# Re-ordered first loads in a fused linear-attention and MLP kernel: parameter rows at the head of the queue, the first batch's k and v as 96 rows of six

## The chip, the cores and the metric

The kernel runs on one core of a Trainium2 chip. The metric is the device time of one execution in microseconds; where several runs are given, their median. The core has five engines that run side by side, each through its own instruction list in order: TensorE (PE) for matmuls, VectorE (DVE), ScalarE (ACT), GpSimd (POOL) and SyncE (SP), which here only issues transfers. ScalarE's list also issues a few. Sixteen DMA engines carry the transfers.

## The reference

Two layers, one after the other. The first is linear attention without a softmax, in 8 batches of 8 heads, 576 positions and a head size of 64; the second a mixer over tokens and then over channels (512 wide, 2048 hidden).

```python
kv  = einsum('bhsd,bhse->bhde', k, v)
o   = einsum('bhsd,bhde->bhse', q, kv)
rms = sqrt(mean(o * o, axis=-1, keepdims=True) + 1e-06)
x   = (o / rms * g_norm)            # heads side by side: [8, 576, 512]

a1  = alpha1 * x + beta1
u   = x + lam * einsum('ts,bsd->btd', w_tok, a1)
a2  = alpha2 * u + beta2
out = u + lam * (maximum(a2 @ w_ch1, 0.0) @ w_ch2)
```

All inputs and the output are float32.

## The kernel before

The work of one batch goes through fixed steps: k'v per head (`kv_first` for batch 0, in float32; `kv_groups` for the others), q times it with the normalisation (`qkv_groups`, L751 for batch 0 and L744 for the others on TensorE, L779 to L808 behind it), the token mix (`tok_first`, L867, for batch 0 in two halves of four heads; `tok_groups`, L836), transposes of the result (`ut_pe`, L902, for batches 0 and 1; DMA transposes later), the first channel matmul (`ch1_groups`, L950 and L964) with its ReLU on ScalarE (L941), and the second (`ch2_groups`, L986), whose result is added to x (L995) and stored. The 576 positions are four chunks of 128 (position 4p + c on partition p in chunk c) and a tail of 64. The batches overlap: while batch b is in its channel matmuls, batch b + 1 is normalised and token-mixed and batch b + 2 has its k'v.

All that is needed once comes ahead of this or between batches 0 and 1. w_tok is loaded, transposed on TensorE (L1117, L1135) and completed by a row of its column sums (L1158). The four blocks of w_ch1 are loaded and cast to bfloat16. The four blocks of w_ch2 are loaded into spare buffers (`stg`, and `kf` for the last) and multiplied by lam (L1221, sixteen products on VectorE or GpSimd, of which the last eight write one common key, `w2s`). lam, alpha1 (times lam and g_norm), g_norm and alpha2 each become a tile of 128 equal rows by a matmul with a row of ones (L1049) and a copy (`lam_bc`, `e1g_bc`, `g_bc`, `a2_bc`).

The first loads: ScalarE's queue issues the 64-position tails of k and v of batch 0 (L497, L1063) and the rows of the parameters (L1020), and alpha2 and beta2 once more as columns of 128x4 (L1026). SyncE's queue issues, for each half of the heads, k, v and q of batch 0 as 128 rows of four positions, then w_tok, w_ch1 and the rest.

No order is written by hand. A planner, the class `Prog`, takes all operations with a cost in microseconds, a priority and their dependencies, and runs through a model of time in which each engine takes the ready operation with the best priority; the order that comes out is written as the instruction lists. A transfer in the model takes its cost `dma_us` on one line of transfers if SyncE issues it, and its cost and 2.3 us alone if ScalarE does. `plan` repeats that six times, moving the priorities of what leads to the first sixteen `ch1` groups, and keeps the best. Until the first `ch1` group is placed, the planner puts a filler into TensorE's list wherever TensorE would otherwise stand in the model: a matmul on zeros whose result nobody reads (L1276). So the fillers are a fixed part of the list, and the list is followed in order, whatever the loads do on the chip.

Of the kernel before, what the change touches and what calls it, by code (L numbers as in the profile page):

```python
# [6 lines left out]
F32 = mybir.dt.float32  # L7
# [7 lines left out]
NH = 8  # L15
# [32 lines left out]
class Prog:  # L48
# [116 lines left out]
    def schedule(self):  # L165
# [66 lines left out]
        while left:  # L232
            progressed = False
            for e, q in queues.items():
                while q and free[e] <= t + 1e-9:
# [157 lines left out]
def bass_transnormer_attn__then__resmlp_affine_kernel(  # L393
# [15 lines left out]
    with ExitStack() as stack:  # L409
# [34 lines left out]
        vt0 = stg[:, 2, 0, :].rearrange("p (h d) -> p h d", h=NH)  # L444
# [16 lines left out]
        wst2 = hst[0:64, 2304:2880]  # L461

# [26 lines left out]
        def load_main(tile, key, src, b, hs, eng="SP"):  # L489
# [4 lines left out]
                dma_us=4.0 * (hs.stop - hs.start) / 8)  # L494

        def load_tail(tile, key, src, b, lo, eng="SP"):
            P.op(eng, 0.6, lambda e: e.dma_start(  # L497
                tile[lo:lo + 64, :, :], src[b, :, 512:576, :].rearrange("h s d -> s h d")),
                w=[key], dma_us=0.8)

        HALVES = (slice(0, 4), slice(4, 8))
        ALL = (slice(0, 8),)

# [92 lines left out]
        def kv_first():  # L596

            def group(a):
                t = P.ptile(1)

                def f(e):
                    for c in range(5):
                        for h in range(4 * a, 4 * a + 4):
                            o = t.flat(slice(64 * (h % 2), 64 * (h % 2) + 64))[
                                :, 64 * (h // 2 - 2 * a):64 * (h // 2 - 2 * a) + 64]
                            m = e.matmul(o, kf[:, h, c, :] if c < 4 else kft[0:64, h, :],
                                         vf[:, h, c, :] if c < 4 else vt0[0:64, h, :],
                                         start=(c == 0 and h < 4 * a + 2), stop=(c == 4),
                                         skip_group_check=True)
                    return m  # L610
                P.op("PE", 1.6, f, r=[("kf", a), ("vf", a), "kft", ("stg", 2)], w=[t])
# [364 lines left out]
        def ch2_groups(b):  # L976
# [31 lines left out]
            for c, n in order:  # L1008
# [4 lines left out]
        params = ((g_norm, prow2[:, 0:64], g_bc, "g"), (moe_alpha1, prow[:, 0:512], e1g_bc, "e1"),  # L1013
                  (moe_lam, prow[:, 512:1024], lam_bc, "lam"),
# [3 lines left out]
        def load_rows():  # L1018
            for src, row, dst, key in params:
                P.op("AQ", 0.5, lambda e, s=src, d=row: e.dma_start(d, s[None, :]),  # L1020
                     w=[key + "r"], dma_us=0.05)

        def load_params():
            def column(e, i, src):
                with nc.allow_non_contiguous_dma(reason="tiny parameter columns"):
                    return e.dma_start(ab2[:, i, :], src.rearrange("(j p) -> p j", p=128))  # L1026
# [282 lines left out]
```

## Time and profile before

| | |
|---|---|
| median of 3 runs | 384.19 us (383.81 to 384.56) |
| profiled execution | 382.44 us |
| its span in the profile | 380.5 us, 6099 instructions |
| TensorE matmuls busy | 366.6 us (96%) |
| VectorE busy | 215.4 us (57%) |
| ScalarE busy | 180.4 us (47%) |
| GpSimd busy | 94.0 us (25%) |
| transfers | 59.28 MB in 94837 packets |

In the views of the profile, times count from the start of the span. A row of a timeline or a group names the engine, the line of the kernel, the operation, what is written and what is read, and how many instructions are taken together. PE is a matmul, PEld the loading of its weights, SPq and ACTq the issuing of a transfer. A float32 matmul of one instruction in the list shows as two passes where the instruction is no transpose. A busy share is that of issued work: a filler counts like any matmul.

### The profile page before, as it was taken

What the parts mean: (1) busy time and instruction counts of PE and PEld (TensorE: products, weight loads), DVE (VectorE), ACT (ScalarE), POOL (GpSimd) and SP (SyncE); (2) the same over time, 40 slices, a digit from 0 to 9 for tenths busy, and PEclk for the clock granted to TensorE, in tenths of its full rate; (3) what the DMA queues carried; (4) which work ended last, traced back from release to release, by engine and by line L of the source; (5) the groups of instructions that cost most, each with busy time, mean ns of one, the idle gap of its engine ahead of it and who ended that gap; (6) DMA issues with size and microseconds to landing.
All of it is one profiled execution on the core that took longest, in us unless ns stands there. A gap on an engine that the chain in (4) does not pass through costs nothing.

```text
span 380.5 us, 6099 instructions
## 1 busy us (share of the span) xinstructions
PE 366.6 (96%) x2660; PEld 216.6 (57%) x2414; DVE 215.4 (57%) x318; ACT 180.4 (47%) x284; POOL 94.0 (25%) x77
## 2 busy tenths in 40 slices
PE   5999999997999999999999999999999999999995
PEld 2686856545765465446764464447764554447642
DVE  2348688998594457595647248574826256720021
ACT  1359578803893239703872069406750078007500
POOL 4014450690073200610064002410342006200000
PEclk9699999999999999999999999999999999999999
DMA  8999999549999859685965339342703210220012
GB/s 198 315 358 251 329 290 293 126 140 261 264 205 244 150 164 276 140 125 157 287 125 140 110 106 271 67 97 84 138 2 87 81 28 2 55 96 29 2 68 70
DMA packets 94837, 59.28 MB, mean 156 GB/s; under 512 B 61334, under 2 KB 85910, under 8 KB 94682
## 3 DMA queue, kind: packets, MB, share of 16 engines
q1 hardware_dynamic: 92688, 58.62, 62.0%
q10 hardware_dynamic: 2122, 0.27, 0.6%
q8 instruction: 20, 0.33, 0.4%
q14 instruction: 7, 0.06, 0.0%
HBM read 38.04 MB, written 9.44 MB: 125 GB/s over the span
## 4 chain that ended last, share of the span: by engine, by line
PE 89%; DVE 6%; ACT 2%; DMA 2%; issue 1%; ACTq 0%
PE ps L986 29%; PE ps L964 18%; PE ps L950 14%; PE ps L836 8%; PE ps L665 4%; PE ps L744 2%; PE ps L387 2%; DMA xm<-in_moe_lam_dram 2%; PE ps L1276 2%; PE ps L629 1%; PE ps L867 1%; PE ps L751 1%; PE ps L1049 1%; PE ps L902 1%; DVE qs L559 1%; ACT ht L941 1%
## 5 line engine op out<-in xcount | busy, mean ns | idle before, releaser
L986 PE MATMUL ps<-w,ht 128*128 128x512 bf16 x561 | 127.1, 379 | 0.8
L941 ACT ACTIVATE ht<-ps,hb 128x512 bf16<-128x512 f32 (+1 forms) x128 | 92.9, 740 | 40.1 <-PE ps L964 32.1
L808 POOL TENSOR_TENSOR xm<-xm,g_bc 128x512 f32<-128x512 f32 (+1 forms) x36 | 51.0, 1416 | 173.1 <-DVE rt L804 170.6
L986 PEld LDWEIGHTS ps<-w,ht 128*128 128x128 bf16 x576 | 55.4, 98 | 65.0 <-DVE w L1221 0.3
L964 PE MATMUL ps<-a2t,w 128*128 128x320 bf16 x512 | 72.0, 299 | 0.1
L964 PEld LDWEIGHTS ps<-a2t,w 128*128 128x128 bf16 x512 | 49.2, 98 | 20.7 <-ACT ht L941 0.9
L950 PE MATMUL ps<-a2t,w 128*128 128x512 bf16 x246 | 56.4, 379 | 0.5
L995 DVE TENSOR_TENSOR xm<-ps,xm 128x512 f32<-128x512 f32 x32 | 21.9, 690 | 60.0 <-PE ps L986 59.8
L681 ACT ACTIVATE kvd<-ps 64x128 bf16<-64x128 f32 x28 | 7.6, 272 | 89.9 <-PE ps L665 89.7
L950 PEld LDWEIGHTS ps<-a2t,w 128*128 128x128 bf16 x256 | 24.2, 98 | 27.2
L781 DVE TENSOR_REDUCE small<-sq 128x16 f32<-128x1024 f32 (+3 forms) x27 | 25.2, 935 | 22.4 <-ACT sq L779 22.2
L836 PE MATMUL ps<-rt,wt 128*128 128x512 bf16 x135 | 35.2, 379 | 1.2 <-DVE xm L995 0.9
L843 DVE TENSOR_TENSOR xm<-ps,xm 128x1024 f32<-128x1024 f32 x14 | 17.0, 1220 | 21.6 <-PE ps L836 21.6
L836 PEld LDWEIGHTS ps<-rt,wt 128*128 128x128 bf16 x140 | 13.6, 98 | 17.2 <-DVE xm L995 1.4
L779 ACT ACTIVATE sq<-ps 128x1024 f32<-128x1024 f32 (+3 forms) x27 | 21.5, 800 | 3.6 <-PE ps L751 2.6
L559 DVE TENSOR_TENSOR qs<-qf,qs 128x2048 bf16<-128x2048 f32 (+1 forms) x10 | 17.3, 1751 | 6.5 <-ACT qs L486 6.5
L665 PE MATMUL ps<-vr,kr 128*128 128x256 f32 x140 | 21.0, 297 | 0.0
L804 DVE TENSOR_TENSOR rt<-xm,e1g_bc 128x1024 bf16<-128x1024 f32 (+1 forms) x18 | 20.8, 1162 | 0.1
L849 POOL TENSOR_TENSOR a2b<-xm,a_bc 128x512 bf16<-128x512 f32 x8 | 11.1, 1394 | 38.9 <-DVE xm L843 38.7
L800 DVE TENSOR_TENSOR xm<-ps,small 128x1024 f32<-128x1024 f32 (+1 forms) x18 | 19.9, 1104 | 0.7 <-DMA out_dram<-xm 0.3
L744 PEld LDWEIGHTS ps<-kvd,qt 128*128 128x128 bf16 x280 | 17.8, 98 | 3.7
L665 PEld LDWEIGHTS ps<-vr,kr 128*128 128x128 f32 x140 | 18.4, 190 | 1.6
(110 smaller groups left out, 341.2 us busy)
## 6 DMA issues: line engine op xcount, KB each, us to landing
out_dram<-xm SPq DMA_DIRECT2D x32, 256.0 KB, 2.4
kf<-in_k_dram SPq DMA_DIRECT2D x7, 1024.0 KB, 6.1
vf<-in_v_dram SPq DMA_DIRECT2D x7, 1024.0 KB, 9.3
qf<-in_q_dram SPq DMA_DIRECT2D x7, 1024.0 KB, 8.8
stg<-in_moe_w_ch_dram SPq DMA_DIRECT2D x5, 1024.0 KB, 16.5
ht<-in_moe_w_tok_dram SPq DMA_DIRECT2D x1, 1152.0 KB, 11.5
kf<-in_k_dram SPq DMA_DIRECT2D x2, 512.0 KB, 8.0
vf<-in_v_dram SPq DMA_DIRECT2D x2, 512.0 KB, 9.3
```

Of the source, the lines that this page charges most:

```text
L559: lambda e, hi=hi, lo=lo, src=src: e.tensor_tensor(out=lo, in0=src, in1=hi, op=ALU.subtract), r=kin + kh, w=kl, port=True)
L665: m = e.matmul(o, flat(kr[:, c, 2 * pr:2 * pr + 2, :]), flat(vr[:, c, 4 * a:4 * a + 4, :]), start=(c == 0), stop=(c == 4))
L744: e.matmul(o, w, kvd[:, h, 0, :], start=True, stop=False)
L779: P.op("ACT", act_us(64 * m), lambda e: e.activation(sqv, raw(), ACT.Square), r=[t], w=[("sq", sqs)])
L781: P.op("DVE", dve_us(64 * m), lambda e: e.tensor_reduce(out=smv, in_=sqv.rearrange("p (h d) -> p h d", h=m), axis=AX.X, op=ALU.add), r=[(" ...
L808: P.op("POOL", pool_us(64 * nh), lambda e, xc=xc: e.tensor_tensor(out=xc, in0=xc, in1=g_bc[rows, None, :].to_broadcast([nr, nh, DH]), op=A ...
L836: m = e.matmul(t.ap()[:, i, :], tok_w(b, sc, c), rsrc(b, sc), start=(sc == 0), stop=(sc == 4))
L941: P.op("ACT", act_us(n) + 0.09, lambda e: e.activation(dst, src(), ACT.Relu, bias=hb[:, fj:fj + 1]), r=[t, ("hb", fj // 4)], w=[("ht", fj)])
L950: m = e.matmul(t.flat(), w1[:, dj, 128 * fj:128 * fj + 128], a2t[:, dj, 0:512], start=(dj == 0), stop=(dj == 3))
L964: m = e.matmul(t.ap()[:, i, 0:320], w1[:, dj, 128 * fj:128 * fj + 128], a2t[:, dj, 320 * i:320 * i + 320], start=(dj == 0), stop=(dj == 3))
L986: m = e.matmul(t.flat(), ht[:, fj, 128 * c:128 * c + 128], w2[:, fj, :], start=(fj == 0), stop=(fj == 15))
L995: P.op("DVE", dve_us(512), lambda e: e.tensor_tensor(out=x, in0=t.flat(), in1=x, op=ALU.add), r=[t] + keys, w=keys)
```

## The change

It has five parts.

ScalarE's queue begins with the parameter rows; g_norm and alpha1 come out ahead of the others. The tails of k and v of batch 0 are gone from it. alpha2 and beta2 are no longer loaded as columns but as four rows of 128 each (`abr`), which one TensorE transpose turns into columns.

k and v of batch 0 are loaded as 96 rows of six positions per half of the heads (`load_first`), which covers all 576 positions, so they have no tail. The first half uses the buffers `kf` and `vf`; the second half's k lies in a part of `stg`, its v in the half of `w2` that the first two w_ch2 blocks fill later. `kv_first` takes six chunks of 96 positions in place of four of 128 and one of 64.

The broadcasts of lam and alpha2 (`spread`) are put behind the transposes of w_tok; those of alpha1 and g_norm stay in front.

In the planner's model, transfers of ScalarE's queue now stand in the same line as SyncE's, and the costs of the loads are smaller (3.6 for 4.0, 0.75 for 0.8).

The products of w_ch2 with lam no longer write the common key; each waits for the readers of the buffer that its own output covers.

```diff
                     if pick.lat is not None:
-                        if e == "SP":
-                            dma_free = max(dma_free, t) + pick.lat
-                            pick.end = dma_free + 2.0
-                        else:
-                            pick.end = t + pick.lat + 2.3
+                        dma_free = max(dma_free, t + 0.3) + pick.lat
+                        pick.end = dma_free + 2.0
...
+        def six(key, a):
+            if a == 0:
+                ap = {"k": kf, "v": vf}[key][0:96].rearrange("p h c d -> p (h c d)")
+            elif key == "k":
+                ap = stg[0:96, 2].rearrange("p j c -> p (j c)")
+            else:
+                ap = w2[0:96, 0:8].rearrange("p j c -> p (j c)").bitcast(F32)
+            return ap[:, 0:1536].rearrange("p (h c d) -> p h c d", h=4, c=6)
...
-                dma_us=4.0 * (hs.stop - hs.start) / 8)
+                dma_us=3.6 * (hs.stop - hs.start) / 8)
...
-                w=[key], dma_us=0.8)
+                w=[key], dma_us=0.75)
...
+        def load_first(a):
+            for key, src in (("k", k), ("v", v)):
+                P.op("SP", 0.6, lambda e, src=src, key=key: e.dma_start(
+                    six(key, a).rearrange("p h c d -> p h (c d)"),
+                    src[0, HALVES[a], :, :].rearrange("h (p c) d -> p h (c d)", c=6)),
+                    w=six_keys(key, a), dma_us=2.05)
...
-                    for c in range(5):
-                        for h in range(4 * a, 4 * a + 4):
+                    ks, vs = six("k", a), six("v", a)
+                    for c in range(6):
+                        for h in range(4):
...
-                            m = e.matmul(o, kf[:, h, c, :] if c < 4 else kft[0:64, h, :],
-                                         vf[:, h, c, :] if c < 4 else vt0[0:64, h, :],
-                                         start=(c == 0 and h < 4 * a + 2), stop=(c == 4),
+                            m = e.matmul(o, ks[:, h, c, :], vs[:, h, c, :],
+                                         start=(c == 0 and h < 2), stop=(c == 5),
...
-        params = ((g_norm, prow2[:, 0:64], g_bc, "g"), (moe_alpha1, prow[:, 0:512], e1g_bc, "e1"),
-                  (moe_lam, prow[:, 512:1024], lam_bc, "lam"),
+        abr = xtl[0:8, 1, 64:192]
+        params = ((moe_lam, prow[:, 512:1024], lam_bc, "lam"),
+                  (moe_alpha1, prow[:, 0:512], e1g_bc, "e1"), (g_norm, prow2[:, 0:64], g_bc, "g"),
...
+            for i, src in enumerate((moe_alpha2, moe_beta2)):
+                P.op("AQ", 0.5, lambda e, i=i, s=src: e.dma_start(
+                    abr[4 * i:4 * i + 4, :], s.rearrange("(j p) -> j p", p=128)),
+                    w=[("abr", i)], dma_us=0.05)
...
-            for i, src in enumerate((moe_alpha2, moe_beta2)):
-                P.op("AQ", 0.5, lambda e, i=i, s=src: column(e, i, s), w=[("ab2", i)],
-                     dma_us=0.5)
-            P.op("DVE", 0.1, lambda e: e.tensor_copy(out=b2c[:], in_=ab2[:, 1, :]),
-                 r=[("ab2", 1)], w=["b2c"])
+            t = P.ptile(1)
+            P.op("PE", 0.1, lambda e: e.transpose(t.flat()[:, 0:8], abr[0:8, :], ident[0:8, 0:8]),
+                 r=["ident", ("abr", 0), ("abr", 1)], w=[t])
+            P.op("DVE", 0.2, lambda e: e.tensor_copy(
+                out=ab2[:].rearrange("p i j -> p (i j)"), in_=t.flat()[:, 0:8]),
+                r=[t], w=[("ab2", 0)])
+            P.op("DVE", 0.2, lambda e: e.tensor_copy(out=b2c[:], in_=t.flat()[:, 4:8]),
+                 r=[t], w=["b2c"])
...
+            spread(("e1", "g"))
+
+        def spread(names):
+            late = [] if "g" in names else [("wtm", sc) for sc in range(5)]
             for src, row, dst, key in params:
-                if dst is None:
+                if key not in names:
                     continue
...
-                P.op("PE", 1.0, lambda e, row=row, t=t, n=n: e.matmul(
+                P.op("PE", 1.05 if n > 64 else 0.2, lambda e, row=row, t=t, n=n: e.matmul(
                     t.flat()[:, 0:n], ones[:], row, start=True, stop=True),
-                    r=["ones", key + "r"], w=[t])
+                    r=["ones", key + "r"] + late, w=[t])
...
         load_rows()
-        load_tail(kft, "kft", k, 0, 0, "AQ")
-        P.op("AQ", 0.6, lambda e: e.dma_start(
-            vt0[0:64], v[0, :, 512:576, :].rearrange("h s d -> s h d")),
-            w=[("stg", 2)], dma_us=0.8)
         for i, hs in enumerate(HALVES):
-            load_kv(0, hs, False)
+            load_first(i)
             load_q(0, hs, False)
...
         run([wt_groups()])
+        spread(("lam", "a2"))
+        free_rows()
...
                 for hh in range(4):
+                    P.readers.setdefault(("w2p", n, hh), []).extend(
+                        P.readers["w2s" if n > 1 else "w2l"])
                     P.op(dve_pool(512), 0, lambda e, hh=hh: e.tensor_tensor(
                         out=w2[:, 4 * n + hh, :], in0=s_[:, hh], in1=lam_bc[:],
-                        op=ALU.mult), r=sk + ["lam"], w=[("w2p", n, hh)] + ["w2s"] * (n > 1), pri=60, port=True)
+                        op=ALU.mult), r=sk + ["lam"], w=[("w2p", n, hh)], pri=60, port=True)
```

More of the change, by code (lines that the diff above doesn't have):

```diff
@@ L461, in bass_transnormer_attn__then__resmlp_affine_kernel, with six_keys @@
         wst2 = hst[0:64, 2304:2880]
+        def six(key, a):
[6 more added lines that the diff above has]
+            return ap[:, 0:1536].rearrange("p (h c d) -> p h c d", h=4, c=6)
+        def six_keys(key, a):
+            if a == 0:
+                return [(key + "f", 0), (key + "f", 1)]
+            return [("stg", 2)] if key == "k" else ["w2l"]
         def flat(ap):
```

16 lines of the change are left out of this document (7 added, 9 removed).

## The prediction

> **What bounds the kernel now.** I read the page's head and its slices, then the chain that ended last, then stretches of the first 100 us. The head and three slice rows of the page:
>
> ```profile
> span 380.5 us, 6099 instructions
> ...
> PEclk9699999999999999999999999999999999999999
> DMA  8999999549999859685965339342703210220012
> ```
>
> One slice is 9.5 us. The clock that TensorE is granted is low in one slice only, the second. The DMA engines are full for seven slices, so the start is the only place where loads can rule. Busy time by stretch (columns: stretch, its length, busy us and count of PE, PEld, DVE, ACT, POOL, then granted clock, DMA share, GB/s):
>
> ```profile
> 6.70:9.20 2.50, 0.02 (x1) 0.00 (x0) 0.00 (x0) 0.00 (x0) 0.00 (x0) 1.00 1.15 267
> 9.20:12.20 3.00, 2.76 (x44) 2.02 (x44) 2.72 (x4) 0.71 (x2) 0.00 (x0) 0.98 1.26 203
> 12.20:18.90 6.70, 6.70 (x54) 4.71 (x51) 0.46 (x2) 2.33 (x5) 0.00 (x0) 0.50 1.10 364
> 18.90:48.30 29.40, 29.06 (x313) 23.13 (x316) 20.17 (x43) 20.01 (x45) 10.59 (x13) 1.00 1.10 314
> ...
> 68.60:96.00 27.40, 24.50 (x133) 13.35 (x132) 25.84 (x30) 9.64 (x17) 15.14 (x9) 1.00 0.67 175
> ...
> 117.20:380.00 262.80, 257.47 (x1708) 143.85 (x1531) 134.03 (x187) 110.23 (x164) 47.84 (x35) 1.00 0.47 113
> ```
>
> From 117 us on TensorE is busy 98% of the time, and the order of its work there is the same in both kernels but for groups moved by a few matmuls. So the time of the whole is the time at which that steady part begins. Ahead of it stand two weak places: the start (an empty stretch of 2.5 us, then 6.7 us at half clock) and 68 to 96 us, where VectorE is nearly full and TensorE lacks 2.9 us. The chain in the start (start, us, what):
>
> ```profile
> 2.95 6.26 DMA xm<-in_moe_lam_dram
> 9.25 1.29 PE ps L1049 x4
> 10.73 1.58 PE ps L606 x40
> ...
> 14.31 3.61 PE ps L629 x32
> ...
> 18.97 1.05 PE ps L1049 x2
> ...
> 23.66 1.90 PE ps L629 x32
> ...
> 35.07 2.40 PE ps L1276 x11
> ```
>
> The row of lam holds up the first broadcast, and from there on TensorE's own order is the chain, up to the first channel-mixer matmul (L950). What stands in it from 10 us on that computes nothing are the fillers of L1276 (groups of a stretch, and three rows of the timeline):
>
> ```profile
> L1276 PE MATMUL ps<-a2b 128*128 128x512 bf16 x25 | 6.2, 379 | 0.3 <-issue 0.2
> ```
> ```profile
> 1.86 4.86 PE L1276 MATMUL ps<-a2b 128*128 128x512 bf16 x14 [1.86 <-DVE a2b L1077]
> ...
> 34.94 2.53 PE L1276 MATMUL ps<-a2b 128*128 128x512 bf16 x11
> 48.33 0.38 PE L950 MATMUL ps<-a2t,w 128*128 128x512 bf16 x1
> ```
>
> (28 fillers are written out there; three records are missing. Their weight loads are all in the trace.)
>
> **The change part by part.** *Rows first.* The two 128 KB tails of k and v leave ACT's queue; g_norm and alpha1 go first on it. TensorE's order becomes 6 fillers, the g broadcast, 18 fillers, then k'v of the first four heads. Landings, from issue (last column):
>
> ```profile
> kf<-in_k_dram SPq DMA_DIRECT2D x1, 512.0 KB, 5.1
> vf<-in_v_dram SPq DMA_DIRECT2D x1, 512.0 KB, 7.1
> ...
> ab<-in_moe_beta_dram ACTq DMA_DIRECT2D x1, 2.0 KB, 9.7
> ```
> ```profile
> 0.75 0.72 ACTq L497 DMA_DIRECT2D kft<-in_k_dram  x1
> ...
> 1.25 0.49 SPq L490 DMA_DIRECT2D vf<-in_v_dram  x1
> ```
>
> lam took 6.26 us and beta2's column 9.7 us because they stood behind the tails in one queue. g at the head of it should take at most kf's 5.1 us, which moved 512 KB in that; 512 KB at the 267 GB/s of the first stretch is 2.0 us, so about 3.1 us is left: it lands at 0.75 + 3.1 = 3.9. Six cold fillers end at 1.86 + 6 x 0.43 = 4.4 (the 14 took 4.86 us, eight of them cold), so g should cost no wait; at 5.1 us it would land at 5.9 and cost 1.5. The 14 fillers end at 6.7, ten more at 2.53/11 = 0.23 each and g's two passes (0.33, from 9.25's four in 1.29) give 9.35. k and v are now 576 KB a half: v landed at 1.25 + 7.1 = 8.35; all of that stretched by 576/512 gives 9.2. So k'v starts at 9.35, where it started at 10.73: **1.4 us** gained; between -0.1 (g late) and 1.4.
>
> *The clock.* The empty 2.5 us goes: fillers reach up to the data. The stretch at half clock (6.70 us x 0.5) loses **3.35 us** of work; the same 32 passes of L629 take 3.61 there and 1.90 later. I take all of it; the ends are 0 and 3.35. [...] The row shows the drop, so I keep it.
>
> *k and v as 96x6 rows.* A group of k'v is 24 matmuls in place of 20, so 48 passes for 40 (1.58 us): 0.3 each if all passes cost alike, but the tails' passes were the dearer ones; **-0.3 us** for both, between -0.6 and 0. In transfers, 1024 tail packets and 1024 four-byte packets of the two columns leave, which moves later loads up by 1 to 2 us; nothing is taken for it, for TensorE's order, not the loads, is the chain after 10.7 us. beta2 and alpha2 as rows cost one small transpose and a copy: **-0.1**.
>
> *Broadcasts.* lam's goes from ahead of k'v into the stretch: **-1.1** (two passes, 1.05 at full clock, row 18.97). a2's stays in it, moved behind the first x transposes. e1's stays ahead; it waits for VectorE's three products of rows, which themselves wait for lam and beta1, some 3 us from an issue at about 3, so done by 9; it is due at 13.5.
>
> *A new order.* The planner's cost of a load falls from 4.0 to 3.6 and all order up to the third batch moves. Half of the first token mix (25 matmuls, half of L867) now stands between the transposes of w_tok and their sums, where fillers stood, and 13 fillers are left of 28 behind the first k'v: 15 x 0.22 = 3.3 us. If the waits that they covered are still there, nothing is gained; if none is, 3.3. w_tok is among what they covered:
>
> ```profile
> 10.80 0.50 SPq L1074 DMA_DIRECT2D ht<-in_moe_w_tok_dram  x1
> ```
> ```profile
> ht<-in_moe_w_tok_dram SPq DMA_DIRECT2D x1, 144.0 KB, 10.3
> ```
>
> It landed at 21.1. Adding up the new order from 9.35 by the rows above, TensorE comes to it at about 24, so that wait is gone. Those for the sums' copies and for the second half's normalised rows I cannot bound as closely, and take half: **1.7**.
>
> So the first L950 starts 1.4 + 3.35 - 0.3 - 0.1 - 1.1 + 1.7 = 4.95 us earlier, at about 43.4.
>
> *Whether later loads allow that.* They go on at the DMA engines' pace. Batch 1's v and the last block of w_ch2:
>
> ```profile
> 34.48 0.69 SPq L490 DMA_DIRECT2D vf<-in_v_dram  x1
> ```
> ```profile
> vf<-in_v_dram SPq DMA_DIRECT2D x1, 1024.0 KB, 9.3
> ...
> kf<-in_moe_w_ch_dram SPq DMA_DIRECT2D x1, 1024.0 KB, 11.2
> ```
> ```profile
> 50.26 2.35 DVE L487 CAST vr<-vf 128x1024 fp32r<-128x1024 f32 x2
> ...
> 51.35 1.28 SPq L1217 DMA_DIRECT2D kf<-in_moe_w_ch_dram  x1
> ```
> ```profile
> 71.16 1.28 POOL L1221 TENSOR_TENSOR w<-kf,lam_bc 128x512 bf16<-128x512 f32 x1
> ```
>
> v is there at 43.8 and cast at 50.3; the block at 62.6 and used at 71.2. Both have 6 us and more, so 5 us fit.
>
> *The products w_ch2 x lam.* They no longer write a common key, so the last eight may run side by side. Waits, and the chain at the second weak place:
>
> ```profile
> POOL w L1221 <- DVE w L1221: 13.2, 1, 13.2
> ```
> ```profile
> PE ps L902 <- DVE xm L843: 1.9, 1, 1.9
> ```
> ```profile
> 78.80 1.66 DVE w L1221
> ...
> 80.48 1.64 DVE w L1221
> ...
> ...
> 89.78 1.24 DVE xm L843
> ...
> 91.06 1.97 PE ps L902 x16
> ```
>
> GpSimd stood 13.2 us for VectorE there, and two products (3.3 us) sit in VectorE's chain that holds TensorE up. In the new order GpSimd takes all four of the last block, and 15 k'v matmuls of batch 2 stand ahead of the transposes that waited. TensorE can get back the 2.9 us that it lacked and no more; behind GpSimd's two more products stand the products with g_norm that VectorE's additions wait for, so a loss is possible: two at 1.28 is 2.6. Between -2.6 and 2.9; I take half of the gain, **1.4**, since both moves are on that chain.
>
> Sum: 4.95 + 1.4 = 6.35 us. The profiled execution took 382.44 us, 1.9 more than its span of 380.5, and the median of the runs is 384.19, 1.75 above it. Taken off the median: 384.2 - 6.35 = **377.8 us**.
>
> **Rivals.** (1) *The front is gained and given back.* The stage at 68 to 96 us keeps VectorE's and GpSimd's pace: instead of +1.4 it costs its 2.6, and fillers turn into waits (-1.7): 6.35 - 4.0 - 1.7 = 0.65, so 383.5. For it: VectorE's 25.84 of 27.4 us. Against: GpSimd's 13.2 us of standing go.
>
> (2) *The clock drops all the same*, or its drop was an accident: 377.8 + 3.35 = 381.2. For it: the clock fell three us after work had come back, so thin work counts; the new start has single waits for g, k and q. Against: none is near 2.5 us. [...]
>
> (3) *96 rows load slower.* If a load on 96 of 128 partitions goes at 96/128 of the rate, v's 8.35 becomes 8.35 x 1.125 x 1.33 = 12.5 and k'v starts 1.8 us later than before, not 1.4 earlier: 381.0. Nothing in the trace has 96 partitions. [...]
>
> (4) *Slower: TensorE stands for g.* All 18 fillers are queued behind its broadcast. Landing at L, k'v starts at L + 0.3 + 8 x 0.43 + 10 x 0.23 = L + 6. With the 9.7 us of beta2's column, L is 10.45 and k'v starts at 16.5, 7.1 later than reckoned: 384.9. It decides from L of 9.7 on (there the 6.35 are gone). For it: lam's row and beta2's column took 6.26 and 9.7 us on that queue. Against: both stood behind tails. The same price holds for any wait of 6 us and more that the new order puts into TensorE's queue.
>
> **How the numbers follow.** The forecast has 0.60, (1) 0.13, (2) 0.08, (3) 0.07, (4) and its like 0.12. Its own range is 374.8 (fillers and stage at their upper ends: 3.1 more) to 380.5 (both terms nil). For 8 in 10 the range goes up to take in (1), (2) and (3), to 383.5. Within 0.2% (0.8 us, about what a measurement tells from no change) falls part of (1) and (4): 0.06; slower keeps 0.10; faster 0.84.
>
> **What would show it.** Right: the granted clock is full from 7 us on; k'v starts at 9 to 10 us; lam's and g's rows land before 6 us; the first channel-mixer matmul starts at 42 to 45 us; GpSimd's long wait for VectorE is gone, and the steady part starts about 6 us earlier. Wrong: a wait of TensorE for a row's load over 2 us, a second stretch at half clock, k or v of the first half landing after 10 us, or a first channel-mixer matmul at 43 us with the steady part where it was.

## The result and the profile after

The changed kernel takes 378.66 us (median of 4 runs, 378.34 to 380.46); the kernel before took 384.00 beside it (median of 4, 383.02 to 384.56). The ratio is 0.9873, with a 95% interval of 0.9835 to 0.9911. The profiled execution took 378.97 us. 377.8 was predicted. Some executions of a kernel run about 5 us longer at a lower granted clock (of the kernel before, 388.26 to 389.01 us at 0.972 or 0.973, where most took 381.74 to 384.66 at 0.985 to 0.991); the ratios leave out those recorded as slow, the medians do not.

The head and two slice rows of the page, and two stretches in the columns of before:

```profile
span 377.2 us, 6108 instructions
...
PEclk9999899999999999999999999999999999999999
DMA  8999999879997869375947249152604110220012
```
```profile
6.70:9.20 2.50, 2.50 (x14) 1.01 (x12) 0.96 (x2) 0.00 (x0) 0.00 (x0) 1.00 1.11 241
12.20:18.90 6.70, 6.26 (x99) 5.01 (x97) 2.50 (x8) 3.17 (x6) 0.00 (x0) 1.00 1.11 264
42.00:62.00 20.00, 19.60 (x159) 11.71 (x151) 15.12 (x28) 15.07 (x28) 6.49 (x5) 0.91 1.10 297
62.00:92.00 30.00, 28.14 (x202) 15.94 (x169) 27.99 (x34) 15.74 (x23) 16.55 (x10) 1.00 0.91 234
```

The empty stretch before 9.2 us is gone, and from 12.2 to 18.9 us the clock is full. In its place the clock is below full (0.91) somewhere between 42 and 62 us. From 62 to 92 us VectorE is busy 27.99 of 30 us.

TensorE's timeline in the start, and the first channel matmul (L967 there, L950 before):

```profile
4.54 0.69 PE L1075 MATMUL ps<-xtl,ones 1*128 1x64 f32 x2
...
9.15 1.62 PE L624 MATMUL ps<-vf,kf 96*64 96x64 f32 x48
...
43.25 5.92 PE L967 MATMUL ps<-a2t,w 128*128 128x512 bf16 x20
```

g's broadcast follows the fillers without a wait, k'v starts at 9.15 us, and the first channel matmul comes 48.33 - 43.25 = 5.08 us earlier. The steady part, however, starts only 3.88 us earlier. The row is the second group of four in batch 2's token mix, of before and of after:

```profile
118.46 1.03 PE L836 MATMUL ps<-rt,wt 128*128 128x512 bf16 x4
```
```profile
114.58 1.03 PE L853 MATMUL ps<-rt,wt 128*128 128x512 bf16 x4
```

So 1.2 us of what the front gained was lost between 43 and 114 us. GpSimd's wait of 13.2 us for VectorE is gone; what it waits for there now are its loads:

```profile
POOL w L1250 <- DMA stg<-in_moe_w_ch_dram: 18.7, 3, 13.1
```

The first loads of after, from issue to landing in the last column:

```profile
kf<-in_k_dram SPq DMA_DIRECT2D x1, 576.0 KB, 5.6
vf<-in_v_dram SPq DMA_DIRECT2D x1, 576.0 KB, 7.7
```
```profile
stg<-in_k_dram SPq DMA_DIRECT2D x1, 576.0 KB, 11.9
w<-in_v_dram SPq DMA_DIRECT2D x1, 576.0 KB, 13.7
```

k and v of the first half are issued at 0.73 and 1.19 us and land at 6.3 and 8.9 us, those of the second half at 14.9 and 17.5 us, and batch 1's v at 45.3 us. Before, they landed at 5.8, 8.3, 14.1, 15.5 and 43.8 us. The loads became later, not earlier. The chain of waits that ended last, followed from the start of the changed kernel, has a load as its longest piece ahead of TensorE's work, q of the second half:

```profile
5.01 14.77 DMA qf<-in_q_dram
19.83 1.99 PE ps L646 x32
```

In the kernel before, TensorE came to these transposes at 23.59 us and did not wait.

### The profile page after: what moved, and what is told of

Same layout as the page of the kernel before. It is cut to its first block, busy times and chain, and to the rows that moved or that the text cites. A ratio compares the mean times of both kernels' runs of the same rounds, so it can differ in the third digit from the quotient of the medians.

```text
span 377.2 us, 6108 instructions
## 1 busy us (share of the span) xinstructions
PE 365.0 (97%) x2672; PEld 214.9 (57%) x2426; DVE 218.3 (58%) x324; ACT 181.0 (48%) x281; POOL 91.6 (24%) x75
## 4 chain that ended last, share of the span: by engine, by line
PE 77%; DVE 12%; DMA 6%; ACT 1%; SPq 1%; issue 1%
PE ps L1003 29%; PE ps L981 16%; PE ps L967 12%; PE ps L853 9%; DMA qf<-in_q_dram 4%; PE ps L682 3%; DMA out_dram<-xm 2%; DVE qs L576 2%; DVE w L1250 2%; PE ps L761 2%; PE ps L384 2%; PE ps L884 1%; DVE xm L817 1%; DVE small L798 1%; PE ps L919 1%
## 5 line engine op out<-in xcount | busy, mean ns | idle before, releaser
L825 POOL TENSOR_TENSOR xm<-xm,g_bc 128x512 f32<-128x512 f32 (+1 forms) x36 | 52.1, 1447 | 169.6 <-DVE rt L821 166.1
L967 PE MATMUL ps<-a2t,w 128*128 128x512 bf16 x246 | 57.6, 386 | 0.5
L967 PEld LDWEIGHTS ps<-a2t,w 128*128 128x128 bf16 x256 | 24.6, 99 | 28.5 <-issue 2.2
L798 DVE TENSOR_REDUCE small<-sq 128x16 f32<-128x1024 f32 (+3 forms) x27 | 25.1, 936 | 22.0 <-ACT sq L796 21.8
L761 PEld LDWEIGHTS ps<-kvd,qt 128*128 128x128 bf16 x280 | 17.8, 98 | 3.8
L496 ACT ACTIVATE qs<-qf 128x2048 bf16<-128x2048 f32 (+1 forms) x8 | 12.6, 1583 | 13.3 <-DMA qf<-in_q_dram 13.3
```

The source lines that it names most:

```text
L761: e.matmul(o, w, kvd[:, h, 0, :], start=True, stop=False)
L798: P.op("DVE", dve_us(64 * m), lambda e: e.tensor_reduce(out=smv, in_=sqv.rearrange("p (h d) -> p h d", h=m), axis=AX.X, op=ALU.add), r=[(" ...
L825: P.op("POOL", pool_us(64 * nh), lambda e, xc=xc: e.tensor_tensor(out=xc, in0=xc, in1=g_bc[rows, None, :].to_broadcast([nr, nh, DH]), op=A ...
L967: m = e.matmul(t.flat(), w1[:, dj, 128 * fj:128 * fj + 128], a2t[:, dj, 0:512], start=(dj == 0), stop=(dj == 3))
```

## The experiments

All times are medians, and a ratio is to the kernel before, run beside it on the same chip. Three times of each profiled execution carry the reading: the first channel matmul, VectorE's first reduction for batch 1 (L781 before, L798 after), and the second group of batch 2's token mix, which is where the steady part begins (262 to 263 us from there to the end in all of them).

| | first channel matmul | reduction, batch 1 | token mix, batch 2 | time | ratio (95%) |
|---|---|---|---|---|---|
| before | 48.33 | 67.80 | 118.46 | 384.00 | |
| after | 43.25 | 66.13 | 114.58 | 378.66 | 0.9873 (0.9835 to 0.9911) |
| e1, after again | 43.23 | 64.72 | 113.18 | 377.45 | 0.9849 (0.9820 to 0.9878) |
| e2, loads over 128 rows | 42.40 | 66.77 | 115.23 | 379.56 | 0.9894 (0.9863 to 0.9925) |
| e3, thin fillers | 43.65 | 65.20 | 113.66 | 379.62 | 0.9913 (0.9880 to 0.9945) |
| e4, tails added | 44.41 | 66.99 | 115.46 | 382.17 | 0.9955 (0.9915 to 0.9996) |
| e5, products in a chain | 42.65 | 63.20 | 112.63 | 377.17 | 0.9846 (0.9818 to 0.9874) |
| e6, e2 with e5 | 41.56 | 62.02 | 111.12 | 375.33 | 0.9805 (0.9776 to 0.9834) |
| e7, GpSimd later still | 42.39 | 64.58 | 114.62 | 377.75 | 0.9855 (0.9826 to 0.9884) |
| e8, before without the key | 49.68 | 70.93 | 123.23 | 386.02 | 1.0078 (1.0045 to 1.0110) |
| e9, before with ten fillers | 45.30 | 64.78 | 117.04 | 381.73 | 0.9968 (0.9944 to 0.9992) |
| e10, two heads side by side | 43.38 | 66.91 | 115.37 | 379.90 | 0.9907 (0.9883 to 0.9931) |
| e11, e10 with e5 | 43.30 | 62.95 | 112.03 | 377.06 | 0.9845 (0.9822 to 0.9868) |
| e12, e11 with fewer fillers | 41.61 | 61.58 | 110.66 | 375.11 | 0.9780 (0.9756 to 0.9804) |

Each edit leaves the order of every engine's instruction list as it is, but for what its diff adds or cuts.

### e1: the changed kernel again

No edit.

> The changed kernel itself, unaltered, once more, to stand beside the next three. Both theories: the first channel-mixer matmul at about 43.3 us again, time about 378.7 us. Theory A (loads: after the first channel-mixer matmul VectorE's chain waits for batch 1's loads, which come 2 to 3 us later than before because the 96-row loads are slow): executions differ little, whatever their granted clock. Theory B (clock: the eight matmuls at half clock at 43 us lose what was gained): executions with a granted clock of 1.000 are faster by 1.5 us or more than those at 0.995.

It took 377.45 us (376.39 to 378.15). The granted clock of this execution reads full throughout (1.000). In the profile of after it does not; its windows from 42 us on (granted clock, DMA share and GB/s are the last three columns), and those of e1:

```profile
42.00:43.00 1.00, 0.89 (x30) 0.82 (x28) 1.00 (x2) 0.87 (x3) 0.00 (x0) 0.87 1.27 206
43.00:44.00 1.00, 1.00 (x3) 0.29 (x2) 0.32 (x1) 0.53 (x2) 0.00 (x0) 0.50 1.18 180
44.00:46.00 2.00, 2.00 (x6) 0.73 (x5) 0.63 (x2) 0.69 (x1) 0.00 (x0) 0.50 1.13 237
```
```profile
42.00:43.00 1.00, 0.94 (x34) 0.89 (x33) 0.80 (x2) 0.87 (x3) 0.00 (x0) 1.00 1.26 189
43.00:44.00 1.00, 0.99 (x5) 0.48 (x5) 0.55 (x1) 0.76 (x2) 0.00 (x0) 1.00 1.14 232
44.00:46.00 2.00, 2.00 (x11) 0.88 (x9) 1.59 (x3) 1.37 (x2) 0.00 (x0) 1.00 1.06 276
```

The same list at the same place ran at half clock in one execution and not in the other. It cost 66.13 - 64.72 = 1.4 us at the reduction, and as much at batch 2's token mix. Without it the steady part starts 118.46 - 113.18 = 5.28 us earlier than before, 0.2 more than the first channel matmul's 5.10. The stage behind the front thus keeps the gain but adds next to nothing.

The front itself holds a surprise. The 18 fillers ahead of the first k'v took 5.19 us here and 4.06 in after, so k'v starts 1.12 us later than the 9.15 of after:

```profile
10.27 1.62 PE L624 MATMUL ps<-vf,kf 96*64 96x64 f32 x48
```

The first channel matmul is nevertheless at the same place (43.23 and 43.25), because near 20 us TensorE waits in both for q of the second half (0.45 us here, 0.65 in after). Theory B asked for 1.5 us or more between executions at the full clock and those at 0.995. The four of after took 378.35 us at 1.000, 378.34 at 0.999, 378.97 at 0.995 and 380.46 at 0.993, so the times bear it out only in part.

### e2: the first loads over 128 partitions

Each load of k and v keeps its bytes but is spread over 128 rows of 288 elements per head. The matmuls read the first 96 rows, so k'v is not the reference's; it is the loads that are tested.

```diff
...
-                    six(key, a).rearrange("p h c d -> p h (c d)"),
-                    src[0, HALVES[a], :, :].rearrange("h (p c) d -> p h (c d)", c=6)),
+                    wide(key, a),
+                    src[0, HALVES[a], :, :].rearrange("h s d -> h (s d)").rearrange(
+                        "h (p x) -> p h x", x=288)),
...
```

> Same instruction order on every engine; only the four first loads of k and v bring the same 576 KB as 128 rows of 1152 bytes per head instead of 96 rows of 1536. k and v then lie in the wrong layout and the output is not the reference's; no instruction is added or left out. Theory A: v of the first half lands about 0.5 to 1 us earlier, q of the second half at about 17.5 instead of 19.8 us, batch 1's v at 43 instead of 45.4, and the time falls by 1 to 2 us to about 377. Theory B: loads come earlier, the time stays within 0.5 us of the changed kernel's.

The loads landed much earlier: k and v of the first half at 4.9 and 6.5 us, of the second at 11.4 and 13.1, batch 1's v at 40.6. Between 1 and 9 us the DMA engines were as busy but moved more; the windows of after and of e2:

```profile
1.00:9.00 8.00, 7.13 (x26) 2.91 (x26) 2.76 (x9) 1.49 (x2) 4.28 (x8) 1.00 0.92 205
```
```profile
1.00:9.00 8.00, 7.13 (x22) 2.81 (x23) 4.65 (x11) 1.49 (x2) 4.28 (x8) 1.00 0.94 257
```

The first channel matmul came 0.8 us earlier than in e1, and yet the kernel was 2.1 us slower, which nothing expected of it explains. The place shows in the timelines of VectorE and GpSimd, first e1's, then e2's:

```profile
51.64 1.29 DVE L1250 TENSOR_TENSOR w<-stg,lam_bc 128x512 bf16<-128x512 f32 x2
...
54.75 3.57 DVE L576 TENSOR_TENSOR qs<-qf,qs 128x512 bf16<-128x512 f32 x4
...
59.56 5.24 DVE L1250 TENSOR_TENSOR w<-stg,lam_bc 128x512 bf16<-128x512 f32 x5
64.72 2.33 DVE L798 TENSOR_REDUCE small<-sq 128x16 f32<-128x1024 f32 x2
```
```profile
53.89 4.65 DVE L586 TENSOR_TENSOR qs<-qf,qs 128x512 bf16<-128x512 f32 x4 [0.28 <-ACT qs L505]
...
59.78 7.07 DVE L1261 TENSOR_TENSOR w<-stg,lam_bc 128x512 bf16<-128x512 f32 x5
66.77 2.33 DVE L809 TENSOR_REDUCE small<-sq 128x16 f32<-128x1024 f32 x2
```
```profile
54.99 3.00 POOL L1261 TENSOR_TENSOR w<-stg,lam_bc 128x512 bf16<-128x512 f32 x2 [2.49 <-DMA stg<-in_moe_w_ch_dram]
59.39 6.31 POOL L1261 TENSOR_TENSOR w<-kf,lam_bc 128x512 bf16<-128x512 f32 x4 [1.40 <-DMA kf<-in_moe_w_ch_dram]
```

VectorE works here without a gap, and its list is the chain that batch 1's normalisation waits in. Five products of w_ch2 with lam take it 5.24 us in e1 and 7.07 in e2 (1.05 and 1.41 each), where the two at 51.64 in e1, with GpSimd at rest, take 1.29 (0.65 each). In e2 the earlier loads let GpSimd run its own four beside all of VectorE's five. The reductions, 1.2 us each, are no slower beside GpSimd (e1) than after its products have ended (e2). That gave a new theory, C: VectorE's stage from 43 to 90 us is the chain, and what it reads from two tiles in SBUF slows down while GpSimd multiplies beside it. The key that the change took away had kept the two apart.

### e3: thin fillers

The 18 fillers behind g's broadcast are cut to one column each, so that the empty stretch ahead of the first k'v comes back.

```diff
...
-            return e.matmul(t.flat(), wz[:, 0:128], wz, start=True, stop=True)
+            fillers[0] += 1
+            n = 1 if 6 < fillers[0] < 25 else 512
+            return e.matmul(t.flat()[:, 0:n], wz[:, 0:128], wz[:, 0:n], start=True, stop=True)
```

> Same order; the 18 fillers between g's broadcast and the first k'v get one column in place of 512, so TensorE is nearly empty from 5 to 9 us. The output is not affected. If the empty stretch was what took the clock before: half clock for 6 to 7 us somewhere between 9 and 20 us, the first channel-mixer matmul 3 us later than in the changed kernel, time 380 to 382. If the clock's drop before was an accident: no half-clock stretch, and the time as in the changed kernel.

```profile
8.89 2.83 PE L624 MATMUL ps<-vf,kf 96*64 96x64 f32 x48 [3.09 <-DMA vf<-in_v_dram]
12.19 3.01 PE L646 MATMUL ps<-ident,qf 128*64 128x128 f32 x32 [0.47 <-issue]
```

After 3.09 us of standing, k'v takes 2.83 us where it took 1.62, and the q transposes 3.01 where they took 1.97: 2.25 us lost. (The granted clock doesn't show it: its mean over this execution is 0.999, where 2.25 us lost at half clock would make it 0.994. The slow matmuls show only in their durations.) The first channel matmul is only 0.4 us later than in e1. Most of the loss was made up at once: k'v starts at 8.89 us, as soon as v is there, and in e1 at 10.27 behind its fillers, and e1's wait of 0.45 us for q near 20 us is gone. So the slow stretch came as expected of the first case, but not the 3 us and the 380 to 382. The time is 2.2 us above e1's; the profile shows 0.5 of that at batch 2's token mix, and where the rest goes I can't say. Behind the full fillers the first k'v takes 1.62 us and not 2.83, but in e1 they also end about 1 us after v has landed (9.28 us).

### e4: the tails again

ACT's queue loads the two 128 KB tails once more, into buffers that are not used yet.

```diff
+        for i, src in enumerate((k, v)):
+            P.op("AQ", 0.0, lambda e, i=i, s=src: e.dma_start(
+                sq[0:64, i, 0:512].rearrange("p (h d) -> p h d", h=NH),
+                s[0, :, 512:576, :].rearrange("h s d -> s h d")),
+                w=[("sq", i)], pri=-5000, dma_us=0.0)
```

> Same order; two 128 KB loads of 64 tail positions of k and v (into a scratch buffer, not used) are put back at the head of ScalarE's queue, ahead of the parameter rows. If queueing behind them is what made lam's row take 6.3 us: g lands after 6 us, TensorE stands for it 2 to 3 us behind the first six fillers, k'v starts at 11 to 12 us, the first channel-mixer matmul is 2 to 3 us later and the time 380 to 382. If rows are slow for another reason: g's landing and the time as in the changed kernel.

The run missed its aim: in the order that came out the two loads stood behind the rows, at 2.83 and 3.54 us, so it doesn't show rows behind tails. g and the first k'v were where they are in after (4.53 and 9.18 us). The second k'v moved to 19.87 us because v of the second half landed at 19.8 (17.8 in e1) and the reused buffer held up ScalarE, and the time rose to 382.17. It shows only that 256 KB more in the first stretch cost 4 to 5 us, of which the profile has 2.3 at batch 2's token mix.

### e5: the products in a chain again

The last eight products of w_ch2 wait for each other as before the change; every list stays as it is.

```diff
...
+        one = sorted(last8[8:], key=lambda o: (o.start, o.idx))
+        for y, o in zip(one, one[1:]):
+            o.deps.add(y)
```

> The new kernel with every instruction list unchanged, but the last eight products of w_ch2 with lam again one after the other, as the common key had them. Theory C (from 43 to 90 us VectorE's list is the chain, and what it does in SBUF slows down while GpSimd multiplies beside it): GpSimd stands until VectorE's five products are done, these take about 0.65 us each in place of 1.05 (3.3 us for 5.24), the reduction of batch 1 starts at about 62.8 us in place of 64.72, and the time falls by 1 to 2 us to about 375.7. Theory D (what GpSimd's standing cost was a loss, and taking the key away was a gain of its own): the time is that of the new kernel (377.45) or higher, since GpSimd ends later (70.5 for 68.6).

```profile
59.85 3.21 DVE L1253 TENSOR_TENSOR w<-stg,lam_bc 128x512 bf16<-128x512 f32 x5
63.20 2.35 DVE L798 TENSOR_REDUCE small<-sq 128x16 f32<-128x1024 f32 x2
...
70.52 2.88 DVE L821 TENSOR_TENSOR rt<-xm,e1g_bc 128x1024 bf16<-128x1024 f32 x2
```

VectorE's five products take 3.21 us (0.64 each) and the reduction starts 1.5 us earlier than in e1, as C had it, though 0.58 of that is there at the first channel matmul already. The time, 377.17, can't be told from e1's 377.45: C's 375.7 was wrong, and D's number came out. GpSimd now ends at 71.2 us in place of 68.6 and runs beside the products for `rt`, which take 2.88 us where e1 has 2.36. At batch 2's token mix 0.55 us is left of the 1.5, which is no more than the 0.58 of the front.

### e6: both together

e2's loads and e5's chain. The output is again that of e2's layout.

> The kernel of e2 (first loads over 128 rows, so its output is of another layout of k and v) with the same chain of the last eight products. C: VectorE's five products take 3.3 us in place of 7.07, the reduction of batch 1 moves from 66.77 to about 63 us, and the time falls from 379.56 to about 376. D: no change, 379.5, since the earlier loads and not GpSimd made it slower.

375.33 us, 4.2 less than e2 (375.33 to 379.56), with the reduction at 62.02. So e2's loads were not what made it slow: with GpSimd held back, the earlier loads pay (375.33 for e5's 377.17), and with GpSimd beside VectorE they cost (379.56 for e1's 377.45). Here C holds and D falls. The front shows something else: k'v starts at 10.11 us in e2 and 9.27 in e6, and the first channel matmul moves by the same 0.84. With the earlier loads TensorE's own order is the chain there, which it was not between after and e1.

### e7: GpSimd held back further

As e5, but GpSimd's last seven products, from its third on, wait for VectorE's last (the expectation below says fourth).

```diff
...
+        for o in last8[5:]:
+            if o in P.order["POOL"]:
+                o.deps.add(dv)
...
```

> The new kernel with every instruction list unchanged; all of GpSimd's products from its fourth on wait for VectorE's last product and may run side by side with nothing of VectorE's products or of the four products for q ahead of them. C: these four fall from 3.57 to about 2.7 us as well, the reduction of batch 1 starts at about 62 us, GpSimd ends at about 71 us, still ahead of its next work at 72, and the time is 375.0 to 375.7. D: 377.5 or higher.

The products for q fell to 2.50 us, about as expected, but the time is 377.75, D's number and not C's. This profile again has the half clock at 42 to 45 us, which cost some 1.6 us, and GpSimd ends at 74.3, three later than expected, so that `rt` takes 3.47 us (2.36 in e1). Holding GpSimd back only moves the place where the two meet.

### e8: the kernel before without the key

This takes one part of the change alone, and no list moves.

```diff
...
+        for o in last8[8:]:
+            o.deps -= set(last8)
+            o.deps |= old
```

> The kernel before with every instruction list unchanged; only the order that the common key forces on the last eight products is taken out (each waits for the readers of the buffer it covers). The prediction's step: GpSimd's 13.2 us of standing go, and TensorE gets back up to 2.9 us; 1.4 us faster, about 382. C: GpSimd's products move beside VectorE's products for q and its four products (2.6 and 2.50 us, alone there), which become 3.5 to 5 us; no gain, 0 to 2 us slower than before.

Slower: 386.02 beside 383.92, ratio 1.0078 (1.0045 to 1.0110). Part of that is the clock, since e8's executions lie at granted clocks of 0.972 to 0.990. At 0.985 to 0.987 alone, five of e8 took 384.63 to 386.48 us and seven of the kernel before 383.61 to 384.02: still slower. VectorE's timeline, of before and of e8:

```profile
56.44 0.46 DVE L689 COPY kvd<-kvd 64x256 bf16<-64x256 bf16 x2
...
57.59 1.28 DVE L559 TENSOR_TENSOR qs<-qf,qs 128x512 bf16<-128x512 f32 x2
59.07 1.29 DVE L559 TENSOR_TENSOR qs<-qf,qs 128x512 bf16<-128x512 f32 x2 [0.20 <-ACT qs L486]
```
```profile
57.78 2.34 DVE L689 COPY kvd<-kvd 64x256 bf16<-64x256 bf16 x2
60.14 1.88 DVE L487 CAST qs<-qf 128x512 bf16<-128x512 f32 x2
61.94 3.56 DVE L559 TENSOR_TENSOR qs<-qf,qs 128x512 bf16<-128x512 f32 x4
```

GpSimd no longer stands 13.2 us; its products run from 57.4 to 61.4 and from 63.3 to 66.6 us, and beside them a copy takes five times as long and the products for q 3.56 us in place of 2.57. The two products on VectorE's list at 78.80 stay there whatever GpSimd does. Of this profile's 4.77 us at batch 2's token mix the edit's share is 1.78, lost between the first channel matmul and the reduction: 1.35 are there at the first channel matmul already, which the edit doesn't touch, and 1.64 come behind VectorE's stage, where the clock falls to half from 94 to 98 us (the transposes at 94.19 take 3.41 us in place of 1.97). The wait that looked like a loss was cover.

### e9: the kernel before with ten fillers

The 14th filler is followed by ten more, which is the clock term alone.

```diff
...
+            for i in range(11 if fillers[0] == 14 else 1):
+                m = e.matmul(t.flat(), wz[:, 0:128], wz, start=True, stop=True)
...
```

> The kernel before with one thing added: after the 14th filler ten more, so that TensorE is busy up to the landing of lam's row and the empty stretch of 2.5 us goes; nothing else moves. The prediction's clock term by itself: the stretch at half clock (12.2 to 18.9 us) goes, the 32 passes of the q transposes take about 2 us in place of 3.68, the first channel matmul starts 3.35 us earlier (45.0 for 48.33), and the time falls by 2.5 to 3.35 us to about 380.6 to 381.4. Rival: what the front gains is given back by VectorE's and GpSimd's stage behind it; then the first channel matmul still starts at 45 but the time falls by less than 1 us, to 383 or more.

The stretch at half clock is gone (the q transposes take 1.97 us in place of 3.68), the first channel matmul comes 3.03 us earlier and the reduction 3.02. So the term passes through VectorE's stage whole as far as the reduction. The time, 381.73, is 1.55 below 383.28, about half of that and short of the 2.5 to 3.35 that were expected, and batch 2's token mix is 1.42 earlier. In the profile a second half clock took the rest, behind a wait that the kernel before has as well (one execution, at a granted clock of 1.000, took 378.72); the row of before, and of e9 with its window:

```profile
91.06 1.97 PE L902 MATMUL ps<-ident,xm 128*128 128x128 f32 x16 [1.95 <-DVE xm L843]
```
```profile
88.03 2.92 PE L902 MATMUL ps<-ident,xm 128*128 128x128 f32 x16 [1.95 <-DVE xm L843]
```
```profile
90.00:92.00 2.00, 2.00 (x11) 2.00 (x10) 0.75 (x1) 0.69 (x1) 0.00 (x0) 0.50 1.04 325
```

### e10 and e11: a layout over 128 partitions that computes the same

k and v of two heads lie side by side, 64 rows of nine positions each; k'v has 36 matmuls of 64 rows for 24 of 96. e11 has e5's chain as well.

```diff
...
-                    src[0, HALVES[a], :, :].rearrange("h (p c) d -> p h (c d)", c=6)),
+                    src[0, HALVES[a], :, :].rearrange("(g h) (p c) d -> (h p) g (c d)", h=2, c=9)),
...
-                            m = e.matmul(o, ks[:, h, c, :], vs[:, h, c, :],
+                            m = e.matmul(o, ks[at, h // 2, c, :], vs[at, h // 2, c, :],
```

> The new kernel with the first batch's k and v loaded over all 128 partitions: two heads side by side, 64 rows of nine positions each (2304 bytes a row), so each k'v group has 36 matmuls of 64 rows in place of 24 of 96; the products of w_ch2 as in the new kernel, free of each other. If loads over 128 partitions are the faster ones, k lands before 5 us and v at about 6.5 us. C, as in e2: the earlier loads put GpSimd's products beside VectorE's, which cost 1.4 us each, and the time is about 379 to 380, more than the new kernel's 377.45. Rival (e2 was slow for its own layout's sake): 377 or less.

> The same with the last eight products of w_ch2 one after the other. C: as in e6 (375.33), and 0.3 to 0.8 us more for the k'v groups of 36 matmuls: 375.6 to 376.2, below the new kernel by more than 1 us. Rival: the longer k'v groups cost their full 0.8 us each or more: 377 or more.

v of the first half landed at 6.0 us in both, that of the second at 12.2 and 12.3. e10 took 379.90 us, as C expected, and e11 377.06, which is 0.9 above what C expected and is its rival's number, 377 or more (its profiled execution, 375.91, was within C's). The chain alone was worth 2.8 us; VectorE's rows in e10 and in e11:

```profile
55.84 4.63 DVE L585 TENSOR_TENSOR qs<-qf,qs 128x512 bf16<-128x512 f32 x4
...
61.71 5.28 DVE L1260 TENSOR_TENSOR w<-stg,lam_bc 128x512 bf16<-128x512 f32 x5
```
```profile
54.61 2.50 DVE L585 TENSOR_TENSOR qs<-qf,qs 128x512 bf16<-128x512 f32 x4 [0.63 <-ACT qs L505]
...
59.24 3.21 DVE L1263 TENSOR_TENSOR w<-stg,lam_bc 128x512 bf16<-128x512 f32 x5
```

e11's ratio, 0.9845, is that of e1. The front had not moved: each k'v takes 2.31 us in place of 1.62, as the rival had it, and the first starts at 9.46 us behind its fillers, 3.5 us after its data is there.

### e12: and fewer fillers

e11, with ten of the 18 fillers ahead of the first k'v cut to one column.

```diff
...
-            return e.matmul(t.flat(), wz[:, 0:128], wz, start=True, stop=True)
+            fillers[0] += 1
+            n = 1 if 14 < fillers[0] < 25 else 512
+            return e.matmul(t.flat()[:, 0:n], wz[:, 0:128], wz[:, 0:n], start=True, stop=True)
```

> The kernel of e11 (loads over 128 partitions, last eight products one after the other) with ten of the 18 fillers ahead of the first k'v cut to one column, since v of the first half lands at 6.0 us there and k'v starts only at 9.46. k'v should start at about 7.3 us, the first channel matmul at about 41 (43.30 in e11), and, if VectorE's stage lets it through, the time falls by about 2 us below e11's 377.06, to about 375. Rival: TensorE runs into waits for q, the second half or w_tok that the fillers covered, or VectorE's chain gives the gain back; then 376.5 to 377.5.

375.11 us (374.03 to 375.25), ratio 0.9780 (0.9756 to 0.9804): faster than both kernels, and as expected.

```profile
7.77 2.31 PE L634 MATMUL ps<-vf,kf 64*64 64x64 f32 x72
```

k'v starts at 7.77 us (7.3 expected), the first channel matmul at 41.61 (41).

## Why the prediction was right, and where it was not

The time, 378.66 for 377.8, was right, and likewise the direction and the front's size. Two errors inside the front cancelled, which is luck, and the last term failed. By its steps:

*The start.* k'v at 9.15 us for 9.35 and g without a wait came as said, and the granted clock no longer fell to half there. The clock term is shown by itself in e9: 3.03 us for 3.35. The gain of the first channel matmul was 5.08 us for 4.95, but not by the mechanism that the sum describes. It took TensorE's order, not the loads, for the chain after 10.7 us; in after the chain is the load of the second half's q until 19.8 us, and the 1.12 us between the k'v of after and of e1 make no difference. With the earlier loads of e6, and k'v at 9.27, the first channel matmul comes at 41.56, 6.77 us earlier than before. So the terms (1.4, 3.35, -0.3, -0.1, -1.1 and 1.7) were together about 1.8 us too small: by k'v's 1.46 in e6 and e9's 3.03, the last four, 0.2 together, came to some 2.3. About 1.7 us of waiting for loads, put at nothing, made up for it.

*Loads.* "Moves later loads up by 1 to 2 us" was wrong: they landed 0.5 to 3.7 us later, w_tok's first part the latest (24.0 for 20.3). What holds of rival (3) is the slower rate, which it took as 96/128: from 1 to 9 us the DMA engines moved 205 GB/s with the loads over 96 rows, and 257 (e2) and 275 (e10) with those over 128, that is 0.80 and 0.75 of the rate. Why it is so no run shows. Rival (3)'s price, k'v at 12.5 us, was wrong, since it stretched the whole latency: v landed at 8.9, before the fillers ended. The price of the slower loads was paid later, at q.

*lam's row before 6 us*: wrong. VectorE's first product of rows waits for it until 8.21 us. It was issued at 1.90, so it took 6.3 us with no tails ahead of it, as long as the 6.26 before; queueing behind the tails does not account for its time. Nothing on the chain needs it by then.

*The products w_ch2 x lam, 1.4 us*: this is the step that failed. GpSimd's standing went, as the prediction said, and nothing was gained by it. e1 shows 5.28 - 5.10 = 0.2 us for the whole stage in place of 1.4. From the first channel matmul to the reduction 2.0 us were lost (5.10 gained at the one, 3.08 at the other), because VectorE's products ran beside GpSimd's. About 2.2 came back behind it, where two products of 3.32 us at 78.80 had left VectorE's list. The prediction read the wait as GpSimd's cost and took VectorE's durations as given. The row that it quoted, 1.66 and 1.64 us for one product at 78.80, already showed the slowing: GpSimd multiplies by g_norm beside these two, and stands beside the four at 64.42, which take 0.63 each.

```profile
64.42 2.50 DVE L1221 TENSOR_TENSOR w<-stg,lam_bc 128x512 bf16<-128x512 f32 x4
```
```profile
76.04 7.21 POOL L808 TENSOR_TENSOR xm<-xm,g_bc 128x512 f32<-128x512 f32 x4 [2.24 <-DVE rt L804]
```

With GpSimd's wait put back, 1.4 us were there to be had: from the first channel matmul to batch 2's token mix e11 takes 68.73 us, the kernel before 70.13 and e1 69.95.

What became slower beside GpSimd's products is in the traces: VectorE's products of two tiles in SBUF (0.65 us each alone, 1.41 in e2) and copies within SBUF (0.23 us each alone, 1.17 in e8). The reductions did not: 1.2 us each in e1, beside GpSimd, and in e2, behind it. Nor did the two engines take strict turns: by an estimate from 0.65 and about 1.3 us each alone, e2's five products on VectorE and four on GpSimd would then need about 8.4 us, where about 7.5 pass, so there is some overlap in the records here.

*The clock that drops all the same*, rival (2), came true in part: not in the start, but at 42 us and in some executions only (after and e7, not e1, e5 or e6; the first 20 channel matmuls take 5.92 us in after and 4.48 in those three), at 1.4 to 1.6 us where it was seen. That, and not the stage, is why after's own profile shows 3.88 us in place of 5.28. The rival's other half, that the drop of the kernel before was an accident, is not borne out: in over 60 executions of that kernel the granted clock never lies above 0.991, and one stretch of 6.7 us at half clock makes 0.991 of a span of 380. Whether thin work counts, as the rival had it, no run shows.

*The front given back*, rival (1), had the place right, VectorE's and GpSimd's stage, but of its price only the missing 1.4 us came. The upper end of the forecast's own range, "both terms nil", is 377.8 + 1.7 + 1.4 = 380.9 by its own terms and not 380.5; nothing hangs on that.

What stays open: e3 and e4 are 2.2 and 4.7 us above e1 in the median, and their profiles show 0.5 and 2.3 of it at batch 2's token mix. In e4 a lower granted clock goes with part of the rest: its six longest executions (381.85 to 385.31) lie at granted clocks of 0.988 to 0.996 and its four shortest (379.34 to 379.94) at 0.995 to 0.999. In e3, at 0.997 to 1.000 throughout, it does not. Nor does any run here show what decides where the clock drops.

## What to carry to other kernels

Before a wait of a helper engine is taken out, look at what the chain's engine does during that wait. Here both multiplied tiles in SBUF, VectorE's products took 0.64 us each alone and up to 1.41 beside GpSimd's, and the wait could be what kept the chain fast (e8 lost some 2 us by its removal and e11 won 2.8 by its return, while in e5 the return only moved the place where the two meet). Loads over 96 of 128 partitions were slower by a fifth to a quarter here (205 GB/s for 257 and 275), and fillers that cover a load hide that loss as they hide a gain: when loads come earlier, the fillers have to be shortened too (e12 took 375.11 us for e11's 377.06). Ask the changed kernel for its chain even when the total comes out as forecast: after's showed a load where the sum had TensorE's order.

## What the runs showed of the hardware that was not expected

- VectorE's product of two 128x512 tiles in SBUF takes 0.64 us alone (e5, e11) and, as the mean of five, 1.05 (e1) to 1.41 us (e2) with GpSimd's products beside them; a copy of 64x256 within SBUF took 1.17 us in place of 0.23 (e8). GpSimd's own rise from 1.28 to about 1.55 us (both in e10). Two reductions take 2.33 us with GpSimd at rest (e10) and 2.35 beside its products (e7), and the product of 128x1024 that reads PSUM 1.22 and 1.23.
- The granted clock fell to half at about 42.7 us in after, where TensorE's records show it standing for no more than 0.2 us. What it had just run were 32 matmuls of one column each (0.94 us) and small transposes. The same list kept the clock in e1, so the trigger is not in the list alone.
- The granted clock doesn't show every slow stretch of matmuls: its mean is 0.999 in e3, whose first k'v takes 2.83 us for 1.62, and 1.000 in e1, whose 18 fillers take 5.19 us for 4.06 in after.
